# Last quarter of a fused Fourier and state-space kernel: half of its DMAs on a second queue, its products cut in half, an early table load

## The chip, the cores and the metric

The kernel runs on one core of a Trainium2 chip. The metric is device time in microseconds (us) for one launch: three unprofiled runs of the kernel before took 581.99, 582.04 and 582.89 us (median 582.04). Each core has a matrix engine (TensorE, PE in the profile, with its weight loads as PEld), VectorE (DVE), ScalarE (ACT), GpSimd (POOL) and SyncE (SP). SP, ACT and GpSimd can each issue DMAs; SP and ACT issue on queues that the profile calls hardware_dynamic, GpSimd on one that it calls software_dynamic. The same 16 DMA engines carry all of them.

## The reference

Two heads are computed and set side by side in the output (2048 x 1024, float32).

```python
# head A: real part of a two-dimensional DFT of x (2048 x 512)
a = einsum("bsd,ed->bse", x, dft_hid_re)
b = einsum("bsd,ed->bse", x, dft_hid_im)
y = einsum("ts,bse->bte", dft_seq_re, a) - einsum("ts,bse->bte", dft_seq_im, b)
# head B: S4D convolution of u (2048 x 512) with 128 states a channel
P = exp((A * dt)[:, :, None] * pos)            # A complex, 512 x 128 x 2048
K = 2 * einsum("dn,dnl->dl", C, P).real
y = irfft(rfft(u, 2L) * rfft(K, 2L), 2L)[:L] + u * D_skip
```

## The kernel before

Head A (class `Fnet`) is a chain of large matrix products in float32 accuracy: each float32 operand is split into a high and a low part (`hi` on ACT, `lo` on DVE), and three matmuls of 128x128 by 128x512 (hi·hi, lo·hi, hi·lo, line 369) make one **group of three**. 32 groups of three make one of the last output blocks: eight steps k by four column blocks d, and the last two steps of each d stand together, so that its accumulator can be evacuated on ACT (line 394; the very last one half on ACT, half on DVE, lines 387 to 391) and stored as `out_ya`. The moving operands come as tiles `raw` on SP's queue. There are seven `raw` buffers.

Head B (class `Ssm`) builds the convolution kernel K from tables of powers (lines 611 to 640), for 64 channels at a time (n = 0 to 7). `taps` (line 807) makes 64 channels of K, `stage1_k` does the first step of K's transform on PE (line 838), takes its two PSUM banks off with one ACT copy (line 848) and two DVE operations each (850, 852), and `store_k` writes the result `xk_sb` to DRAM as `xk` in four DMAs of 256 KB: two halves a, each with two halves y. Rows of these stores are 256 bytes long, 1024 rows in a store.

The channels are taken in quarters h of 128. For each quarter and each of four parts q, `load_spectrum` loads the spectra of u and K, `product` multiplies by the second transform step on PE (line 1000, 64 matmuls, two halves r = 0, 1 of 32), copies to SBUF on ACT (line 1014, tile `uk`), forms the complex product on DVE (lines 1017 to 1030, tiles `z` and `uk`), applies the first inverse step on PE (line 1037), copies on ACT (line 1052, tile `z`) and stores `zs` to DRAM (line 1061). `inverse2`, which does the last two quarters, loads `zs` back as `zl` (line 1093: one half of the partitions on SP's queue, the other on GpSimd's), adds and subtracts on DVE (lines 1099, 1101), multiplies by the table `ib2` on PE (line 1108), copies on ACT (line 1113) and stores `out_yb` (line 1116).

In the last quarter (h = 3) the spectra don't fit a tile of their own. They are loaded into the buffers of head A's operand x, eight tiles `x_hi` and `x_lo` for each half r of each q; each DMA for K brings 128 KB in rows of 512 bytes, 256 rows. So K's last store (n = 7), the 16 loads `x_hi<-xk`, `x_lo<-xk` (line 973), the four products of h = 3 and the two inverses of h = 3 form the chain that ends the program, with head A's last two output blocks on PE beside it.

The order of all instructions is written out by a planner (`Plan`): each piece of work is a generator that yields the engine and a planned duration, and the planner always takes the piece that can start first, then the one with the smaller urgency number. The engines then follow that order, each in its own queue. DMAs are issued on SP in that order too. Each of SP's DMAs reports to one of eight semaphores, in turn, so one may have to wait until the DMA eight places earlier on its queue has landed. GpSimd's DMAs have eight semaphores of their own.

Names for what follows: K's last stores are `xk<-xk_sb` for n = 7; the spectra loads are `x_hi<-xk` and `x_lo<-xk`; products q = 0 to 3 are those of h = 3.

Of the kernel before, what the change touches and what calls it, by code (L numbers as in the profile page):

```python
# [56 lines left out]
ASKED, APART_BY, COMES = 2.0, 3.8, 2.4  # L57
APART = None, True
LATE = 1, 1, 3, 1


def HELD():
# [135 lines left out]
class Fnet:  # L198
# [60 lines left out]
    def load_x0(self, raw):  # L259

        yield "dma", load(64)
        self.nc.sync.dma_start(raw[:, :128], self.xin[0, :, :128])
        self.x[0] = self.still(0)
        yield "act", act(128)
        self.nc.scalar.activation(self.x[0][0][:, :128], raw[:, :128], AF.Copy)
        yield "dve", dve(128)
        self.nc.vector.tensor_tensor(self.x[0][1][:, :128], raw[:, :128], self.x[0][0][:, :128].bitcast(F32),
                                     op=OP.subtract)
        self.plan.set(self.x0_ev)
# [164 lines left out]
class Ssm:  # L434


    def __init__(self, tc, ctx, plan, fnet, nd, ldt, dsk, uG, f1u, f1k, w2, ia, ib, ib2, out):
        self.tc, self.nc, self.plan, self.fnet = tc, tc.nc, plan, fnet
        self.nd, self.ldt, self.uG, self.ib2_in, self.out = nd, ldt, uG, ib2, out
        self.const = ctx.enter_context(tc.tile_pool(name="b_const", bufs=1))  # L440
        self.fps = ctx.enter_context(tc.tile_pool(name="b_fps", bufs=1, space=PSUM))
        dram = ctx.enter_context(tc.tile_pool(name="b_dram", bufs=1, space=DRAM))
        self.xu = dram.tile([64, 2, 32, DM], F32, name="xu")
        self.xk, self.zs = (dram.tile([4, 64, 2, 32, PART], F32, name=n) for n in ("xk", "zs"))
        self.dt_dram = dram.tile([128, 4], F32, name="dt_dram")
# [3 lines left out]
        self.cst = [[(n, self.const.tile([128, *a.shape[1:]], F32, name=n), a) for n, a in s] for s in (first, second)]  # L449
# [375 lines left out]
    def stage1_k(self, ks, n, ev):  # L825

        nc = self.nc
        yield ev
        yield "dve", dve(16)
        nc.vector.tensor_tensor(ks[:, 0], self.dskip[:, 16 * n:16 * n + 16], ks[:, 0], op=OP.add)  # L830
        yield self.const_ev
        got = yield from self.banks(2)
        yield "pe", 1.11, None, 64
        for a in range(2):
            for j in range(4):
                for y in range(2):
                    r, o = slice(32 * j, 32 * j + 32), 32 * a + 16 * y
                    nc.tensor.matmul(got[j // 2][1][64 * y:64 * y + 64, j % 2, 256 * a:256 * a + 256], self.f1k[r, a],  # L838
                                     ks[r, o:o + 16].rearrange("p l i -> p (l i)"), start=True, stop=True,
                                     tile_position=(32 * j, 64 * y))  # L840
        self.plan.put(self.kss)
        yield self.xks
        xs = self.tab.tile([128, 2, 16, 64], F32, name="xk_sb")
        for h, (k, p) in enumerate(got):
            even, odd = (p[:, :, 256 * a:256 * a + 256].rearrange("p j (l i) -> p j l i", l=16) for a in range(2))
            lo, hi = (xs[:, a, :, 32 * h:32 * h + 32].rearrange("p l (j i) -> p j l i", j=2) for a in range(2))
            yield "act", act(512)
            nc.scalar.activation(hi, odd, AF.Copy)
            yield "dve", dve(512)
            nc.vector.tensor_tensor(lo, even, hi, op=OP.add)  # L850
            yield "dve", dve(512), *APART
            nc.vector.tensor_tensor(hi, even, hi, op=OP.subtract)
            self.give(k)
        xk = self.xk[n // 2].rearrange("(a s) c (y l) d -> y a (s c) l d", a=2, y=2)[..., 64 * (n % 2):64 * (n % 2) + 64]
        left = [2]
        for a in range(2):
            self.plan.spawn(self.store_k(xk, xs, a, n, left), 1)

    def store_k(self, xk, xs, a, n, left):
        yield "dma", load(512, 230), FAST  # L860
        for y in range(2):
            self.nc.sync.dma_start(xk[y, a], xs[64 * y:64 * y + 64, a])
# [105 lines left out]
    def load_spectrum(self, name, h, q, view):  # L968
        yield "dma", load(512, 270), FAST
        for r in range(2):  # L970
            for p, xt in enumerate(self.xt[h, q][r]):
                n = xt.shape[1]
                self.nc.sync.dma_start(xt[:, :, "uk".index(name)], view[2 * q + r, :, n * p:n * p + n])
        self.plan.set(self.xt_ev[name, h, q])

    def products(self):
        for h in range(4):
            yield self.set_ev[h // 3]
            b = self.sets[h // 3]
            for q in range(4):  # L980
                for n in "uk":
                    yield self.xt_ev[n, h, q]
                yield b.uks
                got = yield from self.banks(2)
                done = Event()
                self.plan.spawn(self.product(b, h, q, got, done), LATE[h])
                yield done

    def product(self, b, h, q, got, done):
        nc, v, a = self.nc, self.nc.vector, self.nc.scalar  # L990
        uk = b.pool.tile([128, 2, 2, 2, 2, PART], F32, name="uk", bufs=b.n)
        yield "pe", 1.89, None, 128
        for r in range(2):
            for c in range(2):
                for xx in range(4):
                    xt = self.xt[h, q][r]
                    xt = (xt[xx * len(xt) // 4])[:, xx % (4 // len(xt))]
                    for g in range(2):
# [2 lines left out]
                                         self.w2[rows, 2 * q + r, xx, 32 * c:32 * c + 32],  # L1001
                                         xt[rows].rearrange("p n d -> p (n d)"),
                                         start=True, stop=True, tile_position=(64 * g, 32 * xx))
        if h < 3:
            self.plan.put(b.xts)
        self.plan.set(done)
        u, t = uk[:, :, :, :, 0], uk[:, :, :, :, 1]
        yield b.zbs
        P = b.pool.tile([128, 2, 2, 2, PART], F32, name="z", bufs=b.n)
        left, ready = [2], Event()  # L1010

        def half(r, k, p):
            yield "act", act(1024), HELD
            a.activation(uk[:, r].rearrange("p g c n d -> p g (c n d)"), p, AF.Copy)  # L1014
            self.give(k)
            yield "dve", dve(512)
            v.tensor_tensor(P[:, r], t[:, r], u[:, r], op=OP.mult)  # L1017
            yield "dve", dve(512), *APART
            v.tensor_tensor(t[:, r], t[:, r], u[:, r, :, ::-1], op=OP.mult)  # L1019
            left[0] -= 1  # L1020
            if not left[0]:
                self.plan.set(ready)
        for r in range(2):
            self.plan.spawn(half(r, *got[r]), LATE[h])
        yield ready
        yield "dve", dve(512)
        v.tensor_tensor(u[:, :, :, 0], P[:, :, :, 0], P[:, :, :, 1], op=OP.subtract)
        self.plan.put(b.zbs)
# [38 lines left out]
    def inverses(self, h):  # L1067

        yield self.zs_ev[h]
        if h >= HALVED:  # L1070
            yield self.ib2_ev
        b = self.sets[int(h >= min(HALVED, 3))]
        for i in range(2):
            yield b.zls
            self.plan.spawn((self.inverse2 if h >= HALVED else self.inverse)(b, h, i, 16), 1)

    def load_ib2(self):
        yield self.set_ev[1]
        yield self.zs_ev[1]
        self.ib2 = self.sets[1].pool.tile([128, 16, 2, 32], F32, name="ib2")  # L1080
        yield "dma", load(512)
        self.nc.sync.dma_start(self.ib2, self.ib2_in)
        self.plan.set(self.ib2_ev)

    def inverse2(self, b, h, i, n):
# [5 lines left out]
        for y, e in enumerate((nc.sync, nc.gpsimd)):  # L1091
            o = n * i + c * y
            e.dma_start(z[64 * y:64 * y + 64], view[:, :, o:o + c])
        yield "dma", load(64 * n, 270), FAST
        t = b.pool.tile([128, c, PART], F32, name="zsum", bufs=b.n)
        for w in range(0, c, 4):
            m = slice(w, w + 4)
# [125 lines left out]
```

## Time and profile before

| what | us |
|---|---|
| median of the unprofiled runs | 582.04 |
| the profiled execution's own time | 583.77 |
| its span (first to last instruction) | 581.9 |
| PE busy in the span | 569.9 (98%) |
| PE's last matmul ends | 576.25 |
| K's last first-step matmuls start | 497.22 |
| first of K's last stores issued | 502.68 |
| first and last spectra load of K issued | 509.56, 524.22 |
| products q = 0 to 3 start on PE | 515.50, 521.03, 531.36, 539.55 |

The profile is of one execution. Its "busy" time for PE counts matmuls that are pipelined, so a busy PE can still be short of its peak; small gaps between matmuls don't show as idle. The chain of work is followed back from the last instruction: at each step to what released it. Times in a timeline count from the span's start, and a row with "xN" merges N instructions.

### The profile page before, as it was taken

What the parts mean: (1) busy time and instruction counts of PE and PEld (TensorE: products, weight loads), DVE (VectorE), ACT (ScalarE), POOL (GpSimd) and SP (SyncE); (2) the same over time, 40 slices, a digit from 0 to 9 for tenths busy, and PEclk for the clock granted to TensorE, in tenths of its full rate; (3) what the DMA queues carried; (4) which work ended last, traced back from release to release, by engine and by line L of the source; (5) the groups of instructions that cost most, each with busy time, mean ns of one, the idle gap of its engine ahead of it and who ended that gap; (6) DMA issues with size and microseconds to landing.
All of it is one profiled execution on the core that took longest, in us unless ns stands there. A gap on an engine that the chain in (4) does not pass through costs nothing.

```text
span 581.9 us, 15684 instructions
## 1 busy us (share of the span) xinstructions
PE 569.9 (98%) x6278; PEld 434.2 (75%) x6278; DVE 523.4 (90%) x927; ACT 371.8 (64%) x729; POOL 42.5 (7%) x64
## 2 busy tenths in 40 slices
PE   8999999999999999999999999999999999999996
PEld 5877777788777777778787776777787778766784
DVE  6999999999999999999999999999989999346723
ACT  5678766673777495758569485844688744344622
POOL 0001101100110000000100001001100000000000
PEclk9999999999999999999999999999999999999999
DMA  7998999997469767867796888469999995699886
GB/s 247 326 362 244 289 287 276 275 285 186 118 162 227 205 172 227 203 172 225 206 223 186 227 200 251 131 173 286 258 287 258 229 289 193 157 227 305 236 198 185
DMA packets 147976, 133.70 MB, mean 230 GB/s; under 512 B 47296, under 2 KB 107328, under 8 KB 147648
## 3 DMA queue, kind: packets, MB, share of 16 engines
q1 hardware_dynamic: 138976, 115.54, 66.6%
q0 software_dynamic: 8640, 16.78, 14.5%
q8 instruction: 49, 0.80, 0.6%
q10 hardware_dynamic: 288, 0.39, 0.2%
q14 instruction: 23, 0.19, 0.1%
HBM read 89.95 MB, written 42.73 MB: 228 GB/s over the span
## 4 chain that ended last, share of the span: by engine, by line
PE 55%; DVE 27%; DMA 7%; issue 6%; ACT 3%; SPq 1%; ACTq 0%; DVEq 0%
PE acc L369 42%; DVE prod L611 9%; DVE t L620 5%; PE f L1000 4%; DVE lo L228 4%; PE f L807 3%; PE f L1037 3%; DMA x_hi<-xk 2%; DMA xt<-xk 2%; DVE t L640 1%; DMA xk<-xk_sb 1%; PE f L838 1%; DVE cs L681 1%; DMA zl<-zs 1%; DVE uk L1019 1%
## 5 line engine op out<-in xcount | busy, mean ns | idle before, releaser
L369 PE MATMUL acc<-hi,x_hi 128*128 128x512 f32 x640 | 258.7, 404 | 0.8 <-ACT x_hi L224 0.7
L369 PE MATMUL acc<-lo,x_hi 128*128 128x512 f32 x640 | 250.8, 392 | 0.0
L369 PE MATMUL acc<-hi,x_lo 128*128 128x512 f32 x640 | 250.2, 391 | 0.0
L611 DVE TENSOR_TENSOR prod<-t,cs 128x1024 f32<-128x1024 f32 (+4 forms) x192 | 163.2, 868 | 1.7 <-ACT t L729 0.6
L369 PEld LDWEIGHTS acc<-hi,x_hi 128*128 128x128 f32 x640 | 120.5, 188 | 50.1 <-issue 23.4
L369 PEld LDWEIGHTS acc<-hi,x_lo 128*128 128x128 f32 x640 | 120.7, 189 | 26.4 <-DVE x_lo L228 0.3
L369 PEld LDWEIGHTS acc<-lo,x_hi 128*128 128x128 f32 x640 | 120.8, 189 | 23.1 <-DVE lo L228 0.2
L224 ACT ACTIVATE hi<-raw 128x512 fp32r<-128x512 f32 x132 | 82.7, 628 | 64.8 <-PE acc L369 48.7
L228 DVE TENSOR_TENSOR lo<-raw,hi 128x512 fp32r<-128x512 f32 x132 | 90.2, 686 | 26.9 <-ACT hi L224 26.9
L620 DVE TENSOR_TENSOR t<-prod 128x512 f32<-128x512 f32 (+4 forms) x192 | 94.3, 512 | 1.0
L627 ACT ACTIVATE square<-t 128x256 f32<-128x256 f32 (+1 forms) x64 | 36.7, 573 | 29.1 <-DVE t L620 26.9
L1014 ACT ACTIVATE uk<-f 128x1024 f32<-128x1024 f32 x32 | 31.3, 1018 | 15.0 <-PE f L1000 15.0
L323 POOL DMA_DIRECT2D lo<-in_sT x28 | 24.5, 874 | 214.8 <-ACT lo L321 44.2
L394 ACT ACTIVATE y<-acc 128x512 f32<-128x512 f32 x47 | 28.0, 595 | 16.6 <-PE acc L369 16.4
L807 PEld LDWEIGHTS f<-t,t 128*32 128x32 f32 x2048 | 29.5, 110 | 6.9 <-issue 4.8
L807 PE MATMUL f<-t,t 128*32 128x64 f32 x2048 | 32.4, 220 | 0.9 <-issue 0.4
L318 POOL DMA_DIRECT2D hi<-in_sT x28 | 15.8, 564 | 190.2 <-PE acc L369 119.8
L1017 DVE TENSOR_TENSOR z<-uk 128x512 f32<-128x512 f32 x32 | 21.9, 686 | 6.1 <-ACT uk L1014 6.0
L1052 ACT ACTIVATE z<-f 128x512 f32<-128x512 f32 x32 | 17.8, 592 | 14.5 <-PE f L1037 11.3
L640 DVE TENSOR_TENSOR t<-square 128x128 f32<-128x128 f32 (+1 forms) x64 | 24.7, 387 | 0.0
L1000 PE MATMUL f<-xt,w 64*32 64x256 f32 x768 | 23.5, 379 | 0.3 <-DMA xt<-xk 0.3
L1019 DVE TENSOR_TENSOR uk<-uk 128x512 f32<-128x512 f32 x32 | 22.1, 691 | 0.9
(102 smaller groups left out, 505.0 us busy)
## 6 DMA issues: line engine op xcount, KB each, us to landing
raw<-in_sT SPq DMA_DIRECT2D x99, 256.0 KB, 5.3
p<-y SPq DMA_DIRECT2D x32, 256.0 KB, 3.5
xk<-xk_sb SPq DMA_DIRECT2D x32, 256.0 KB, 5.1
zs<-z SPq DMA_DIRECT2D x32, 256.0 KB, 4.0
raw<-p SPq DMA_DIRECT2D x32, 256.0 KB, 4.2
hi<-in_sT POOLq DMA_DIRECT2D x28, 256.0 KB, 4.7
lo<-in_sT POOLq DMA_DIRECT2D x28, 256.0 KB, 5.0
xt<-xu SPq DMA_DIRECT2D x24, 256.0 KB, 4.8
```

The source lines that it names most:

```text
L224: self.nc.scalar.activation(hi, src, AF.Copy)
L228: self.nc.vector.tensor_tensor(lo, src, hi.bitcast(F32), op=OP.subtract)
L369: nc.tensor.matmul(acc[d], l[:, cols], r, start=k == 0 and n == 0, stop=k == len(items) - 1 and n == 2)
L394: self.nc.scalar.activation(y, ps, AF.Copy, scale=-1.0 if g[2] == 1 else 1.0)
L611: self.nc.vector.tensor_tensor(p.rearrange("p k d c m -> p k (d c) m"), src.rearrange("p d c l -> p (d c) l")[:, None, :, rows].to_broadca ...
L620: self.nc.vector.tensor_tensor(dst[:, :, :, rows], p[:, 0], p[:, 1, :, ::-1], op=OP.add)
L627: self.nc.scalar.activation(sq, t[:, :, :, m // 2:m], AF.Square)
L640: self.nc.vector.tensor_tensor(t[:, :, 0, m:2 * m:2], box[0][:, :, 0], box[0][:, :, 1], op=OP.subtract)
L807: nc.tensor.matmul(ps[32 * j:32 * j + 32, i], t1[:, d, c], t2[:, d, c], start=c == 0, stop=c == 1, tile_position=(0, 32 * j))
L1000: nc.tensor.matmul(got[r][1][32 * xx:32 * xx + 32, g, 256 * c:256 * c + 256], self.w2[rows, 2 * q + r, xx, 32 * c:32 * c + 32], xt[rows].r ...
L1014: a.activation(uk[:, r].rearrange("p g c n d -> p g (c n d)"), p, AF.Copy)
L1019: v.tensor_tensor(t[:, r], t[:, r], u[:, r, :, ::-1], op=OP.mult)
```

## The change

Seven edits, all but the last of them for the program's last part:

- `store_k`: for n = 7 the half y = 1 of each store goes out on GpSimd's queue (two DMAs), the half y = 0 stays on SP's.
- `load_spectrum`: K's spectra for `x_lo` (p = 1, which only h = 3 has) go out on GpSimd's queue, eight DMAs; those for `x_hi` stay on SP's.
- `stage1_k`: for n = 7 the two banks are taken off by two pieces of work with urgency -1 instead of one after the other.
- `product`: for h = 3 the PE work is given to the planner as two halves of 32 matmuls, and the first half's evacuation is spawned before the second half's matmuls.
- `ib2`, the table of `inverse2`, gets a place of its own that it shares with `f1u` (a table that only the first transform of u uses), and is loaded when the last `t1` table is done instead of after quarter 1's inverse steps.
- `inverses`: the inverses of h = 2 and 3 get urgency 2 instead of 1; the planned load of `zl` is no longer preferred for h = 2.
- `load_x0`: the very first copy (`x_hi`, 128 columns) moves from ACT to DVE.

```diff
@@ load_x0
-        yield "act", act(128)
-        self.nc.scalar.activation(self.x[0][0][:, :128], raw[:, :128], AF.Copy)
+        yield "dve", dve(128, 2)
+        self.nc.vector.tensor_copy(self.x[0][0][:, :128], raw[:, :128])
@@ Ssm.__init__
+        self.ib2 = self.const.tile([128, 16, 2, 32], F32, name="ib2")
+        f1u_at = self.ib2.rearrange("p a b c -> p (a b c)")[:, :64]
...
@@ stage1_k
+        xs = []
+
+        def out(h, k, p):
+            if not xs:
+                yield xs_ev
...
+            yield "act", act(512)
+            nc.scalar.activation(hi, odd, AF.Copy)
+            yield "dve", dve(512)
+            nc.vector.tensor_tensor(lo, even, hi, op=OP.add)
+            yield "dve", dve(512), *APART
+            nc.vector.tensor_tensor(hi, even, hi, op=OP.subtract)
+            self.give(k)
+            left[0] -= 1
+            if not left[0]:
+                self.plan.set(ready)
...
         for h, (k, p) in enumerate(got):
...
+            if n < 7:
+                yield from out(h, k, p)
+            else:
+                self.plan.spawn(out(h, k, p), -1)
+        yield ready
@@ store_k
-        for y in range(2):
-            self.nc.sync.dma_start(xk[y, a], xs[64 * y:64 * y + 64, a])
+        for y, e in enumerate((self.nc.sync, self.nc.gpsimd if n == 7 else self.nc.sync)):
+            e.dma_start(xk[y, a], xs[64 * y:64 * y + 64, a])
@@ load_spectrum
-                self.nc.sync.dma_start(xt[:, :, "uk".index(name)], view[2 * q + r, :, n * p:n * p + n])
+                e = self.nc.gpsimd if p and name == "k" else self.nc.sync
+                e.dma_start(xt[:, :, "uk".index(name)], view[2 * q + r, :, n * p:n * p + n])
@@ product
-        yield "pe", 1.89, None, 128
         for r in range(2):
+            if not r or h == 3:
+                yield "pe", 1.89 if h < 3 else 0.95, None, 128 if h < 3 else 64
...
+            if not r and h == 3:
+                self.plan.spawn(half(0, *got[0]), urgency)
@@ inverses
         if h >= HALVED:
             yield self.ib2_ev
+            yield self.set_ev[1]
...
-            self.plan.spawn((self.inverse2 if h >= HALVED else self.inverse)(b, h, i, 16), 1)
+            self.plan.spawn((self.inverse2 if h >= HALVED else self.inverse)(b, h, i, 16), 1 if h < 2 else AFTER)
@@ load_ib2
-        yield self.set_ev[1]
-        yield self.zs_ev[1]
-        self.ib2 = self.sets[1].pool.tile([128, 16, 2, 32], F32, name="ib2")
-        yield "dma", load(512)
+        yield self.t1_ev[15]
+        yield "dma", load(512), FAST
         self.nc.sync.dma_start(self.ib2, self.ib2_in)
@@ inverse2
-        yield "dma", load(64 * n, 270), FAST
+        yield "dma", load(64 * n, 270), FAST if h == 3 else None
```

The planner's order is the same up to some 85 us before the end, but for the moved copy at the start and the load of `ib2` (its tile is called `ib` in the rows). Where it moves, at three places:

SP's queue around K's last stores, before. `x_hi_6013` to `x_lo_6016` are the four loads of q = 0, `6017` to `6020` those of q = 1, and so on:

```order
L862 DMA xk<-xk_sb 64x16x64 x4
L337 DMA raw<-p_1_3_88 128x512
L403 DMA out_ya<-y 128x512
L973 DMA x_hi_6013<-xk 128x2x128
L973 DMA x_lo_6014<-xk 128x2x128
L973 DMA x_hi_6015<-xk 128x2x128
L973 DMA x_lo_6016<-xk 128x2x128
L973 DMA x_hi_6017<-xk 128x2x128
L973 DMA x_lo_6018<-xk 128x2x128
```

The same place on SP's queue now, down to the last of the `x_hi` loads:

```order
L882 DMA xk<-xk_sb 64x16x64 x2
L339 DMA raw<-p_1_2_87 128x512
L339 DMA raw<-p_1_3_88 128x512
L994 DMA x_hi_6013<-xk 128x2x128
L994 DMA x_hi_6015<-xk 128x2x128
L994 DMA x_hi_6017<-xk 128x2x128
L994 DMA x_hi_6019<-xk 128x2x128
L1121 DMA zl<-zs 64x2x1024 x2
L994 DMA x_hi_6021<-xk 128x2x128
L994 DMA x_hi_6023<-xk 128x2x128
L994 DMA x_hi_6069<-xk 128x2x128
L994 DMA x_hi_6078<-xk 128x2x128
```

GpSimd's queue after its last load for head A, now; before, the two pairs of `zl<-zs` stood there alone:

```order
L882 DMA xk<-xk_sb 64x16x64 x2
L994 DMA x_lo_6014<-xk 128x2x128
L994 DMA x_lo_6016<-xk 128x2x128
L994 DMA x_lo_6018<-xk 128x2x128
L994 DMA x_lo_6020<-xk 128x2x128
L1121 DMA zl<-zs 64x2x1024 x2
L994 DMA x_lo_6022<-xk 128x2x128
L994 DMA x_lo_6024<-xk 128x2x128
L994 DMA x_lo_6070<-xk 128x2x128
L994 DMA x_lo_6079<-xk 128x2x128
L1121 DMA zl<-zs 64x2x1024 x2
```

Ten DMAs went from SP's queue to GpSimd's. SP's half of `zl` for h = 2, which stood behind `ib` and an inverse's store, now stands between the spectra of q = 1 and q = 2, as GpSimd's half does on its own queue. One `out_ya` store that stood ahead of the spectra now stands behind them. Product q = 0 stands two groups of three earlier on PE (23 instead of 25 groups after the last first-step matmuls of K), and between the products stand three groups of three where there were four.

ACT where K's two banks are taken off, before:

```order
L224 ACTIVATE hi<-raw 128x512
L848 ACTIVATE xk_sb<-f_6616 128x2x16x16
L224 ACTIVATE hi<-raw 128x512
L848 ACTIVATE xk_sb<-f_6623 128x2x16x16
L224 ACTIVATE hi<-raw 128x512 x2
```

And now:

```order
L226 ACTIVATE hi<-raw 128x512
L846 ACTIVATE xk_sb<-f_6617 128x2x16x16
L846 ACTIVATE xk_sb<-f_6624 128x2x16x16
L226 ACTIVATE hi<-raw 128x512 x3
L396 ACTIVATE y<-acc 128x512 x3
```

The split of a `raw` tile that stood between the two copies now follows them; on DVE the two operations of the second bank move ahead of that split's `lo` in the same way.

The end of ACT's queue, before:

```order
L394 ACTIVATE y<-acc 128x512 x3
L1113 ACTIVATE zl<-f_7416 128x512 x2
L389 ACTIVATE y<-acc 128x256
L391 DMA out_ya<-y 128x256
L1113 ACTIVATE zl<-f_7470 128x512 x2
```

And now:

```order
L1141 ACTIVATE zl<-f_7382 128x512 x2
L1141 ACTIVATE zl<-f_7429 128x512 x2
L396 ACTIVATE y<-acc 128x512 x3
L391 ACTIVATE y<-acc 128x256
L393 DMA out_ya<-y 128x256
```

The last inverse of head B (`zl`) used to be the last work of all; now seven groups of three of head A follow it on PE, and the program ends with the two stores of half an `out_ya` block.

More of the change, by code (lines that the diff above doesn't have):

```diff
@@ L59 @@
 LATE = 1, 1, 3, 1
+AFTER = 2
+LAST = 1
 def HELD():
@@ L448, in __init__ @@
         second = ("w2", w2), ("ia", ia), ("ib", ib)
-        self.cst = [[(n, self.const.tile([128, *a.shape[1:]], F32, name=n), a) for n, a in s] for s in (first, second)]
+        self.ib2 = self.const.tile([128, 16, 2, 32], F32, name="ib2")
+        f1u_at = self.ib2.rearrange("p a b c -> p (a b c)")[:, :64]
+        self.cst = [[(n, f1u_at if n == "f1u" else self.const.tile([128, *a.shape[1:]], F32, name=n), a) for n, a in s]
+                    for s in (first, second)]
         self.halfpi = self.const.tile([128, 1], F32, name="halfpi")
@@ L832, in stage1_k @@
         got = yield from self.banks(2)
+        xs = []
+        def out(h, k, p):
+            if not xs:
+                yield xs_ev
+            even, odd = (p[:, :, 256 * a:256 * a + 256].rearrange("p j (l i) -> p j l i", l=16) for a in range(2))
+            lo, hi = (xs[0][:, a, :, 32 * h:32 * h + 32].rearrange("p l (j i) -> p j l i", j=2) for a in range(2))
+            yield "act", act(512)
[8 more added lines that the diff above has]
+                self.plan.set(ready)
+        xs_ev, ready, left = Event(), Event(), [2]
         yield "pe", 1.11, None, 64
@@ L842, in stage1_k @@
         yield self.xks
-        xs = self.tab.tile([128, 2, 16, 64], F32, name="xk_sb")
+        xs.append(self.tab.tile([128, 2, 16, 64], F32, name="xk_sb"))
         for h, (k, p) in enumerate(got):
[L845 to L853, printed above, removed]
+            if n < 7:
[3 more added lines that the diff above has]
+        yield ready
+        xs, = xs
         xk = self.xk[n // 2].rearrange("(a s) c (y l) d -> y a (s c) l d", a=2, y=2)[..., 64 * (n % 2):64 * (n % 2) + 64]
@@ L985, in products @@
                 done = Event()
-                self.plan.spawn(self.product(b, h, q, got, done), LATE[h])
+                self.plan.spawn(self.product(b, h, q, got, done), LATE[h] if h < 3 else LAST)
                 yield done
@@ L991, in product, with half @@
         uk = b.pool.tile([128, 2, 2, 2, 2, PART], F32, name="uk", bufs=b.n)
-        yield "pe", 1.89, None, 128
+        u, t = uk[:, :, :, :, 0], uk[:, :, :, :, 1]
+        P, left, ready, urgency = [], [2], Event(), LATE[h] if h < 3 else LAST
+        def half(r, k, p):
+            yield "act", act(1024), HELD
+            a.activation(uk[:, r].rearrange("p g c n d -> p g (c n d)"), p, AF.Copy)
+            self.give(k)
+            if not P:
+                yield P_ev
+            yield "dve", dve(512)
+            v.tensor_tensor(P[0][:, r], t[:, r], u[:, r], op=OP.mult)
+            yield "dve", dve(512), *APART
+            v.tensor_tensor(t[:, r], t[:, r], u[:, r, :, ::-1], op=OP.mult)
+            left[0] -= 1
+            if not left[0]:
+                self.plan.set(ready)
+        P_ev = Event()
         for r in range(2):
+            if not r or h == 3:
+                yield "pe", 1.89 if h < 3 else 0.95, None, 128 if h < 3 else 64
             for c in range(2):
@@ L1006, in product @@
         self.plan.set(done)
-        u, t = uk[:, :, :, :, 0], uk[:, :, :, :, 1]
         yield b.zbs
[L1009 to L1024, printed above, removed]
+        P.append(b.pool.tile([128, 2, 2, 2, PART], F32, name="z", bufs=b.n))
+        self.plan.set(P_ev)
+        for r in range(h == 3, 2):
+            self.plan.spawn(half(r, *got[r]), urgency)
         yield ready
+        P, = P
         yield "dve", dve(512)
```

## The prediction

> **What bounds the kernel now.** The page first, then the busy time by stretch (start:end, length, then busy time and count of PE, PEld, DVE, ACT and POOL, PE's granted clock, share of the DMA engines, GB/s), then the chain of waits. PE is busy nearly all the time, so only what PE waits for, and what stands before its first and after its last matmul, can be won.
>
> ```profile
> span 581.9 us, 15684 instructions
> PE 569.9 (98%) x6278; PEld 434.2 (75%) x6278; DVE 523.4 (90%) x927; ACT 371.8 (64%) x729; POOL 42.5 (7%) x64
> ```
>
> ```profile
> 525.06:576.25 51.19, 51.19 (x678) 37.96 (x674) 28.65 (x44) 22.96 (x37) 1.16 (x2) 1.00 0.82 235
> 576.25:581.90 5.65, 0.00 (x1) 0.00 (x0) 0.00 (x0) 1.08 (x2) 0.00 (x0) 0.88 0.70 206
> ```
>
> PE has no hole from 525.06 on, and 5.65 us follow its last matmul. The chain that ended last, by pieces (start, length), shows a hole ahead of that and what the pieces cost undisturbed:
>
> ```profile
> 512.63 11.17 DMA x_hi<-xk
> ...
> 523.93 1.20 PE f L1000 x32
> 525.13 2.99 PE acc L369 x12
> 528.11 1.05 PE f L1037 x32
> 529.16 2.27 PE acc L369 x9
> 531.43 1.89 PE f L1000 x64
> ...
> 547.82 2.02 PE f L1108 x112
> ...
> 553.17 19.32 PE acc L369 x84
> ```
>
> One load of K's spectra took 11.17 us. A product takes 1.89 us, a group of three (19.32 - 2.27) / 25 = 0.682, and a restart of head A costs 2.99 - 4 x 0.682 = 0.26. PE's timeline gives the waits:
>
> ```profile
> 515.50 0.42 PE L1000 MATMUL f<-x_hi,w 64*32 64x256 f32 x4
> 518.08 0.50 PE L369 MATMUL acc<-hi,x_hi 128*128 128x512 f32 x1
> 521.03 0.64 PE L1000 MATMUL f<-x_hi,w 64*32 64x256 f32 x8
> 522.14 0.42 PE L1000 MATMUL f<-x_lo,w 64*32 64x256 f32 x4 [0.47 <-DMA x_lo<-xk]
> 525.06 0.50 PE L369 MATMUL acc<-hi,x_hi 128*128 128x512 f32 x1
> ```
>
> Product q = 0 took 518.08 - 515.50 = 2.58, q = 1 took 4.03; less 1.89 each that is 0.69 + 2.14 = **2.83 us of waiting**, all of it for K's spectra. (Idle rows show less, because matmuls overlap.) Why they are late, by the queues' timelines and by the DMA view of 513.5 to 520 us:
>
> ```profile
> 502.68 4.67 SPq L862 DMA_DIRECT2D xk<-xk_sb  x4
> 507.44 1.06 SPq L337 DMA_DIRECT2D raw<-p  x1
> 509.56 0.37 SPq L973 DMA_DIRECT2D x_hi<-xk  x1
> 517.89 0.48 SPq L973 DMA_DIRECT2D x_hi<-xk  x1
> 522.11 0.36 SPq L973 DMA_DIRECT2D x_lo<-xk  x1
> 511.58 1.26 POOL L1093 DMA_DIRECT2D zl<-zs  x2 [66.27 <-DMA out_ya<-y]
> ```
>
> ```profile
> q0 software_dynamic: 256, 0.97, 69.0%
> q1 hardware_dynamic: 955, 0.46, 31.9%
> ```
>
> GpSimd's two `zl` loads, in rows of 4 KB, enter at 511.58 and take 0.97 of the 1.43 MB of the next 6.5 us; SP's spectra, in rows of 512 bytes, get 0.46 MB (71 GB/s). And SP's last loads wait for the semaphore of the DMA eight places ahead (517.89 to 522.11).
>
> **The change, part by part.**
>
> *K's stores and loads.* ACT and DVE now take both banks off without the split between them:
>
> ```profile
> 498.38 0.60 ACT L848 ACTIVATE xk_sb<-f 128x512 f32<-128x512 f32 x1 [1.05 <-PE f L838]
> 501.97 0.68 DVE L850 TENSOR_TENSOR xk_sb<-f,xk_sb 128x512 f32<-128x512 f32 x1
> DMA to landing us min/median/max: 4.5/4.8/5.2
> ```
>
> (The last row is the landing of K's four last stores, all from SP.) The second copy can start at 498.98; DVE's four operations of about 0.69 then run from 499.0 and the first stores can go at 501.1 instead of 502.68. The split that waits behind them has groups in hand, at no cost. SP's own loads can't start before the `raw` at 507.44, which waits for a buffer that PE's pace frees: 507.9 against 509.56.
>
> GpSimd's price for such DMAs is not in the trace. Its rows are of 128 rows each:
>
> ```profile
> L323 POOL DMA_DIRECT2D lo<-in_sT x28 | 24.5, 874 | 214.8 <-ACT lo L321 44.2 <-DVE prod L611 33.5 <-DVE t L620 32.3
> L1093 POOL DMA_DIRECT2D zl<-zs x4 | 2.4, 608 | 113.1 <-DMA out_ya<-y 66.3 <-DMA zs<-z 46.8
> 559.10 1.27 SPq L1093 DMA_DIRECT2D zl<-zs  x2
> 559.60 1.27 POOL L1093 DMA_DIRECT2D zl<-zs  x2 [46.77 <-DMA zs<-z]
> ```
>
> After the same release GpSimd starts 0.50 later than SP. A store has 1024 rows, a load 256: if its time is fixed, both cost 0.61; if it goes by rows, 4.9 and 1.22. A gain below 0.61 is excluded, since no row is cheaper. The accumulating form costs 0.27 more for as many rows, so part of the time is work per row; I take the middle, 2.5 and 0.85, being nearest to neither. Then GpSimd's stores are written by 501.1 + 0.5 + 2 x 2.5 = 506.6, the first lands near 508 (501.1 + 0.5 + 2.5 is 504.1, and SP's shortest landing of 4.5 less its issue of about 0.6 is 3.9), and the `x_lo` loads of q = 0 and 1 are written at 508.5 to 511.9, landing from 512 on. PE wants them at 515.50 - 2 x 0.682 = 514.1 and, after 1.89 and 2.27, at 518.3. Both queues now have the spectra of q = 0 and 1 ahead of `zl`; only SP's `zl`, which comes free first, can slow the last `x_lo`. Those of q = 2 stand behind 2 MB of `zl` and are wanted at 518.3 + 1.89 + 2.27 + 1.05 + 2.27 = 525.8, against 531.36 before: by the 230 GB/s of the quoted stretch (235), 2 MB from about 513 end near 522, and the last of them land about 526. I keep **1.0 us of waiting** of the 2.83 (0.5 at q = 1, 0.5 at q = 2). With GpSimd's lower price nothing waits; with the upper, see the rivals. Next late is the store `zs` of q = 0, which now stands behind four `raw` loads, and which the copy of q = 1 waits for:
>
> ```profile
> 538.67 1.08 ACT L1052 ACTIVATE z<-f 128x512 f32<-128x512 f32 x2 [2.39 <-DMA zs<-z]
> ```
>
> It waits 2.39 already; the early load of `ib2` takes 512 KB out of its way, so I add nothing.
>
> [...]
>
> *More switches on PE.* Twelve pieces of head B stand between groups instead of ten: 2 x 0.26, and the inverse of 2.02 cut in two costs about 0.1: **+0.6**.
>
> *The end.* Before, PE's end is followed by two copies and 512 KB of `out_yb`; now by half a copy and 128 KB on two queues.
>
> ```profile
> 576.65 1.08 ACT L1113 ACTIVATE zl<-f 128x512 f32<-128x512 f32 x2 [0.56 <-PE f L1108]
> 577.76 0.38 SPq L1116 DMA_DIRECT2D out_yb<-zl  x1
> DMA to landing us min/median/max: 3.2/3.2/3.2
> 575.71 0.38 ACT L389 ACTIVATE y<-acc 128x256 f32<-128x256 f32 x1 [1.01 <-ACT zl L1113]
> DMA to landing us min/median/max: 3.1/3.4/3.8
> ```
>
> The first landing is that last `out_yb`'s, the second that of the two half `out_ya`. `out_yb` lands at 577.76 + 3.25 = 581.0, 0.9 before the span's end. Now: 0.48 (copy and hop) + 3.1 to 3.8 + 0.9 = 4.5 to 5.2 against 5.65: **-0.8**, in -1.15 to -0.45.
>
> *The start and the table.* Nothing. PE's second group waits for a later tile of x, not for the first copy:
>
> ```profile
> 6.92 0.79 PE L369 MATMUL acc<-hi,x_hi 128*128 128x512 f32 x1 [0.66 <-ACT x_hi L224]
> ACT hi L224 <- PE acc L369: 3.1, 3, 1.7
> ```
>
> The last row, of the waits of 483 to 512 us, covers `ib2`: splits there wait for PE, not for their `raw` loads, so 2 us of DMA among those loads is hidden; without that cover it costs its 512 KB, some 2 us.
>
> **Sum.** -(2.83 - 1.0) + 0.6 - 0.8 = -2.0. The profiled execution took 583.77 (span 581.9), the median is 1.73 lower; carried over: 582.04 - 2.0 = **580.0**.
>
> **The rivals.**
>
> *Nothing lands sooner.* The engines are shared, so the earlier places only make PE wait longer, and it leaves the products when it did: only the end is won against the switches, 582.04 + 0.6 - 0.8 = 581.8, no change. For it: 71 GB/s beside `zl`. Against: q = 0 and 1 are now ahead of `zl`.
>
> *GpSimd's writing goes by rows* (slower). Place: the stores `xk<-xk_sb`. Two at 4.9 end at 501.6 + 9.8 = 511.4; four loads at 1.22 are written at 512.6 to 516.3 and land some 3.2 later, as the half stores above, at 515.8 to 519.5. Product q = 0 then waits about 1.8, q = 1 about 1.9, since SP's `zl` runs beside its `x_lo`, and q = 2 about 1, behind a `zl` that starts at 517: 4.7 instead of 2.83, 582.04 + 1.9 + 0.6 - 0.8 = 583.7. It decides against the change from a price of about 4 us a store. For it: the accumulating row. Against: no row shows more than 0.87.
>
> *`zs` of q = 0 lands later than its reader* and product q = 3 waits 1 to 1.5: 581.2, still faster.
>
> **Chances.** Forecast 0.52, `zs` late 0.06, nothing sooner 0.20, by rows 0.22. Less than 0.2% (1.2 us) can't be told from no change here; so faster 0.58, same 0.20, slower 0.22. The range's low end is no wait at all and the better end: 582.04 - 2.83 + 0.6 - 1.15 = 578.7; its high end takes in the row rival at 583.7.
>
> **What would show it.** Right: GpSimd's rows `xk<-xk_sb` at 1 to 3.5 us; products q = 0 and 1 with under 1 us of waiting together, q = 2 near 526; PE's last matmul at about 575 and under 5.2 us behind it. Wrong: those rows near 5 us, or products that start earlier and last longer by as much, or a new wait at q = 2 or q = 3.

## The result and the profile after

The changed kernel is slower: 587.19 us in the median of 13 runs (584.23 to 589.58) against 582.7 us of the kernel before in 13 runs beside it (581.57 to 585.04). The ratio is 1.0064, with a 95% interval of 1.0046 to 1.0083, or some 3.7 us. (Ratios here and below are estimated over all the runs; the quotient of the two medians would be 1.0077, or 4.5 us.)

The profiled execution took 584.23 us, the fastest of the 13. Its page:

```profile
span 582.5 us, 15689 instructions
PE 570.0 (98%) x6278; PEld 433.5 (74%) x6278; DVE 522.9 (90%) x928; ACT 371.3 (64%) x728; POOL 49.7 (9%) x74
```

The spans can't be set side by side as they stand, since PE's matmuls became fast earlier in this execution. PE's timeline of the kernel before, at the start and at the last first step of K:

```profile
10.07 0.61 PE L369 MATMUL acc<-lo,x_hi 128*128 128x512 f32 x1
10.50 0.42 PE L369 MATMUL acc<-hi,x_lo 128*128 128x512 f32 x1
497.22 1.12 PE L838 MATMUL f<-ks,f1k 32*64 32x256 f32 x32
```

The same view of the kernel after:

```profile
5.04 0.40 PE L371 MATMUL acc<-hi,x_lo 128*128 128x512 f32 x1
495.25 1.12 PE L861 MATMUL f<-ks,f1k 32*64 32x256 f32 x32
```

Matmuls of some 0.40 us, where one still took 0.61 at 10.07 before, begin at 5.04 instead of 10.50, and K's last first step comes 1.97 us earlier. From that step to the end of the span it took 581.9 - 497.22 = 84.68 us before and 582.5 - 495.25 = 87.25 us after: 2.57 us more. PE's timeline there shows where:

```profile
512.17 0.64 PE L1039 MATMUL f<-x_hi,w 64*32 64x256 f32 x8
513.39 0.42 PE L1039 MATMUL f<-x_lo,w 64*32 64x256 f32 x4 [0.58 <-DMA x_lo<-xk]
517.54 0.42 PE L1039 MATMUL f<-x_hi,w 64*32 64x256 f32 x4
527.29 0.65 PE L1039 MATMUL f<-x_hi,w 64*32 64x256 f32 x4 [2.21 <-DMA x_hi<-xk]
530.88 0.50 PE L371 MATMUL acc<-hi,x_hi 128*128 128x512 f32 x1
537.70 0.42 PE L1039 MATMUL f<-x_hi,w 64*32 64x256 f32 x4 [1.16 <-ACT z L1081]
```

Products q = 0 to 3 begin at 512.17, 517.54, 527.29 and 537.70. From q = 0 to q = 1 stand 5.37 us, where a run below without a wait there has 4.18: 1.19 us of waiting. Product q = 2 waits 2.21 us for its spectra and then runs from 527.29 to 530.88, 3.59 instead of 1.89 us, its matmuls at 0.65 instead of 0.40 us. Product q = 3 waits 1.16 us. Together 1.19 + 2.21 + 1.70 + 1.16 = 6.26 us, against 2.83 before. The granted clock stands in the windows around that hole, and the last row is what follows PE's last matmul (columns as in the prediction):

```profile
523.66:527.07 3.41, 1.43 (x7) 0.83 (x5) 1.38 (x3) 0.95 (x2) 0.00 (x0) 1.00 1.05 250
527.07:530.49 3.42, 3.19 (x60) 2.18 (x64) 0.00 (x0) 0.80 (x1) 0.00 (x0) 0.50 1.11 352
578.36:582.50 4.14, 0.00 (x0) 0.00 (x0) 0.42 (x1) 0.38 (x1) 0.00 (x0) 0.90 0.57 199
```

From 0.2 us before the hole's end the granted clock was 0.50, for 3.42 us. The end takes 4.14 us instead of 5.65. GpSimd's timeline tells why the first spectra are late:

```profile
499.66 0.90 POOL L882 DMA_DIRECT2D xk<-xk_sb  x1 [56.45 <-DVE xk_sb L848]
507.68 0.87 POOL L882 DMA_DIRECT2D xk<-xk_sb  x1 [7.12 <-issue]
508.54 2.15 POOL L994 DMA_DIRECT2D x_lo<-xk  x3
512.41 0.72 POOL L994 DMA_DIRECT2D x_lo<-xk  x1 [1.72 <-PE acc L371]
513.26 1.22 POOL L1121 DMA_DIRECT2D zl<-zs  x2
```

A store takes GpSimd 0.90 us, but 7.12 us pass before it starts on the second one, and no semaphore of the trace explains them. The last spectra of K are then late for another reason. The DMA issues of 513.4 to 516.7 us, and the queues from 520 to 526 us:

```profile
zl<-zs POOLq DMA_DIRECT2D x2, 512.0 KB, 12.1
x_hi<-xk SPq DMA_DIRECT2D x4, 128.0 KB, 14.3
x_lo<-xk POOLq DMA_DIRECT2D x4, 128.0 KB, 12.6
```

```profile
q0 software_dynamic: 346, 1.19, 88.0%
q1 hardware_dynamic: 339, 0.17, 15.6%
```

128 KB of spectra took 12.6 to 14.3 us to land, behind 2 MB of `zl`. The two queues moved as many packets each (346 and 339), but GpSimd's hold 3.4 KB on average and SP's 0.5 KB: 1.19 against 0.17 MB. The chain of waits joins the rest together:

```profile
517.73 14.08 DMA out_ya<-y
531.82 5.12 DMA zs<-z
537.05 0.60 ACT z L1081
537.70 1.96 PE f L1039 x64
```

`out_ya` stands behind the spectra, the second of SP's two stores `zs` of q = 0 isn't issued before that landing, ACT's copy of q = 1 waits for the store, and product q = 3 for the copy.

### The profile page after: what moved, and what is told of

Same layout as the page of the kernel before. It is cut to its first block, busy times and chain, and to the rows that moved or that the text cites. A ratio compares the mean times of both kernels' runs of the same rounds, so it can differ in the third digit from the quotient of the medians.

```text
span 582.5 us, 15689 instructions
## 1 busy us (share of the span) xinstructions
PE 570.0 (98%) x6278; PEld 433.5 (74%) x6278; DVE 522.9 (90%) x928; ACT 371.3 (64%) x728; POOL 49.7 (9%) x74
## 4 chain that ended last, share of the span: by engine, by line
PE 46%; DVE 37%; issue 7%; DMA 6%; ACT 1%; SPq 1%; DVEq 0%; ACTq 0%
PE acc L371 36%; DVE prod L616 11%; DVE t L625 6%; DVE lo L230 6%; PE f L1039 3%; PE f L812 3%; DMA out_ya<-y 2%; PE f L1066 2%; DVE t L645 2%; DMA xt<-xu 1%; DVE cs L686 1%; DVE x_lo L230 1%; DVE z L1023 1%; DVE uk L1025 1%; DVE zl L928 1%
```

## The experiments

Two theories and a rival stood at the start. **A**: the 2 MB of `zl`, let in ahead of the spectra of q = 2 and 3, cost. **B**: GpSimd's second store waits for room in a memory that its DMAs need (`dynamic_dma_scratch_size`, 2048 bytes in this program), and that delays all behind it. **C**: the loss lies elsewhere, in the edit at the start for one.

**zl behind the last spectra**

```diff
             yield self.set_ev[1]
+        if h == 2:
+            yield self.xt_ev["k", 3, 3]
```

> The kernel after, with the first inverse's load of 2 MB (zl, both queues) let go only when the last of K's spectra is issued; the order of PE's, ACT's and DVE's instructions stays. Theory A (the 2 MB ahead of the spectra of q = 2 and 3 are what costs): the spectra of q = 2 and 3, which took 12 to 15 us from issue to landing, take under 7; the idle 2.21 us before product q = 2 and the slow matmuls behind it go, q = 3 no longer waits 1.16 us; 3 to 4.5 us less than the kernel after, 0.5 to 2 us less than the kernel before (ratio 0.997 to 0.999). Theory B (GpSimd's queue, whose second store was issued only at 507.68, 7.1 us after the first was written, is what costs): that wait stays, so the loss stays; at most 1 us is won, ratio 1.005 or more. Theory C (the loss is spread over the kernel, by the edit at its start or the table's load): as the kernel after, ratio 1.006.

Measured: 586.92 us, ratio 1.007 (1.0045 to 1.0094): nothing won. The spectra issued from 513.9 to 517.4 did land in time; the waits and the chain show who waited instead:

```profile
x_lo<-xk POOLq DMA_DIRECT2D x5, 128.0 KB, 4.5
x_hi<-xk SPq DMA_DIRECT2D x4, 128.0 KB, 3.2
```

```profile
526.86 11.84 DMA zs<-z
539.45 3.67 PE f L1039 x64
```

```profile
534.00:539.40 5.40, 0.16 (x1) 0.00 (x0) 3.22 (x6) 0.59 (x2) 0.00 (x0) 0.80 0.85 266
539.40:546.00 6.60, 6.55 (x81) 3.74 (x89) 3.07 (x5) 3.17 (x5) 0.00 (x0) 0.65 0.44 123
```

The 2 MB now stand ahead of `zs` of q = 0, which took 11.84 us to land; PE stood still for 5.3 us ahead of product q = 3, which then took 3.67 us. A's mechanism held (3.2 and 4.5 us instead of 14.3 and 12.6), its gain did not: whoever is behind the 2 MB pays.

**More memory for GpSimd's DMAs**

```diff
-    nc = bacc.Bacc(..., dynamic_dma_scratch_size=2048)
+    nc = bacc.Bacc(..., dynamic_dma_scratch_size=2240)
```

Names of runs and expectations say 128 (entries) for 2048 bytes and 140 for 2240; what an entry is, no run shows.

> [...] Theory B: the second store is issued at about 500.6 instead of 507.68, the x_lo loads of q = 0 and 1 land up to 4 us earlier, and what stands behind them too; 2 to 4 us less than the kernel after (ratio 0.999 to 1.003). Theory A: the second store may go earlier, but so do the 2 MB of zl, and the spectra of q = 2 and 3 still take over 10 us behind them; at most 1.5 us less than the kernel after (1.004 to 1.007). [...]

Measured: 582.4 us, ratio 0.9983 (0.996 to 1.0005), just under the range of B (0.999 to 1.003): the loss is gone. GpSimd's and PE's timelines:

```profile
499.24 1.77 POOL L882 DMA_DIRECT2D xk<-xk_sb  x2 [55.98 <-DVE xk_sb L848]
505.11 2.84 POOL L994 DMA_DIRECT2D x_lo<-xk  x4 [4.11 <-DMA xk<-xk_sb]
```

```profile
511.94 0.42 PE L1039 MATMUL f<-x_hi,w 64*32 64x256 f32 x4
516.12 0.42 PE L1039 MATMUL f<-x_hi,w 64*32 64x256 f32 x4
524.55 0.42 PE L1039 MATMUL f<-x_hi,w 64*32 64x256 f32 x4 [0.89 <-DMA x_hi<-xk]
533.52 0.42 PE L1039 MATMUL f<-x_hi,w 64*32 64x256 f32 x4 [1.38 <-ACT z L1081]
```

192 bytes more, and both stores go out one after the other in 1.77 us; the 7.12 us were a wait for room in that memory. The spectra of q = 0 and 1 come in time (511.94 to 516.12 is the 4.18 used above). A shows in what is left: 0.89 for q = 2, 1.38 for q = 3.

**All from SP again**

```diff
-        for y, e in enumerate((self.nc.sync, self.nc.gpsimd if n == 7 else self.nc.sync)):
+        for y, e in enumerate((self.nc.sync, self.nc.sync)):
...
-                e = self.nc.gpsimd if p and name == "k" else self.nc.sync
+                e = self.nc.sync
```

> The kernel after, with K's last stores and all spectra issued from SP again; the rest of the change stays, zl on both queues and ahead of q = 2 and 3 included. Theory A: q = 2 and 3 still stand behind 2 MB; PE waits for them 2 to 4 us, ratio 1.003 to 1.008. Theory B: GpSimd has nothing to wait for; the products wait 2.8 us or less in all, the end keeps its 1.5 us, ratio 0.998 to 1.000.

Measured: 587.69 us, ratio 1.0071 (1.0046 to 1.0097), as the kernel after. GpSimd has nothing to wait for here, so B alone is not the cause of the loss. PE's waits from 495 us on:

```profile
PE f L1039 <- ACT z L1081: 2.9, 1, 2.9
PE f L1039 <- DMA x_lo<-xk: 1.5, 1, 1.5
PE f L1039 <- DMA x_hi<-xk: 0.8, 1, 0.8
```

The spectra make product q = 0 wait, beside GpSimd's half of `zl`, and the copy behind `zs` makes q = 3 wait.

**The edit at the start, alone**

```diff
-        self.nc.scalar.activation(self.x[0][0][:, :128], raw[:, :128], AF.Copy)
+        self.nc.vector.tensor_copy(self.x[0][0][:, :128], raw[:, :128])
```

> The kernel before, with the first copy of x (128 columns) on DVE instead of ACT and nothing else. Theories A and B: no difference, ratio 0.999 to 1.001. Theory C, as far as it means this edit: 2 to 4 us longer. If the edit is what opened PE's clock 5.5 us earlier in the profile of the kernel after (full from 5.0 instead of 10.5 us), the first product of K ends about 2 us earlier, and the ratio is 0.997.

Measured: 583.63 us, ratio 1.0002 (0.9981 to 1.0022): C, as to this edit, is out, and the edit is worth nothing. Nor does it set when the matmuls become fast: with it, those of some 0.40 us began at 5.0 to 7.2 us in the profiles of the kernel after, hold_zl, ring_140 and this run, but at 10.9 in that of no_split. This run also shows how the kernel before spreads: the same order of work, and in this execution

```profile
PE f L1000 <- DMA x_lo<-xk: 2.4, 1, 2.4
```

one hole of 2.4 us where the profiled execution of before had 0.7 and 0.5.

**The early table, alone and undone**

A second theory **A2** took A's place: the table that is loaded early lets the last-but-one quarter's inverse ask for `zl` earlier, SP's half moves from behind `zs` of q = 0 to between the spectra of q = 1 and 2, and whatever stands behind it costs. Its rival **D** was the other order of PE's last pieces. Into the kernel before went the early load alone:

```diff
+        self.ib2 = self.const.tile([128, 16, 2, 32], F32, name="ib2")
...
     def load_ib2(self):
-        yield self.set_ev[1]
-        yield self.zs_ev[1]
-        self.ib2 = self.sets[1].pool.tile([128, 16, 2, 32], F32, name="ib2")
-        yield "dma", load(512)
+        yield self.t1_ev[15]
+        yield "dma", load(512), FAST
```

> The kernel before with one part of the change: ib2 in a buffer of its own (f1u in its first 64 words) and loaded when the last t1 is there, so that the last-but-one quarter's inverse may be asked for earlier. SP's half of the 2 MB of zl then stands between the spectra of q = 1 and 2 (behind all of them before). Theory A2 (it is the early zl that costs, whatever queue the spectra use): PE waits 2 us or more for the spectra of q = 2 or 3 or for the store zs of q = 0, with matmuls of 0.65 us behind the longest hole; 2 to 4.5 us longer than before, ratio 1.003 to 1.008. Theory B (GpSimd's full queue): no store goes from GpSimd here, ratio 0.999 to 1.001. Theory D (the other order of PE's pieces: split last products, inverses asked for less urgently): not in this kernel, ratio 0.999 to 1.001.

Measured: 587.25 us, ratio 1.008 (1.0056 to 1.0104): the whole loss, without GpSimd's stores and without the other edits. The waits of PE from 495 us on:

```profile
PE f L1003 <- DMA x_lo<-xk: 1.6, 2, 1.3
PE f L1110 <- DVE zsum L1101: 1.2, 1, 1.2
PE f L1003 <- DMA x_hi<-xk: 0.6, 1, 0.6
PE f L1110 <- DVE zl L1103: 0.5, 2, 0.3
```

2.2 of these 3.9 us are for spectra, where the profile of before has 1.2 in the same view. In this kernel the early table also put the last inverse behind all groups of head A, where PE waits 1.7 us for DVE, so the run is no clean measure of A2. The other way round, the kernel after with the table late:

```diff
     def load_ib2(self):
-        yield self.t1_ev[15]
-        yield "dma", load(512), FAST
+        yield self.set_ev[1]
+        yield self.zs_ev[1]
+        yield "dma", load(512)
```

> The kernel after with the table ib2 loaded where it was before; spectra and stores still split over SP and GpSimd, with 128 entries. SP's half of zl then stands behind the last spectra and behind zs of q = 0. Theory A2: the spectra of q = 2 and 3 land under 9 us after issue; the 4 us lost come back and some of the end's 1.5 us is kept: ratio 0.997 to 1.001. Theory B: GpSimd's second store still waits to 507 or later, ratio 1.003 or more. Theory D: ratio 1.004 or more.

Measured: 583.04 us, ratio 1.0006 (0.9985 to 1.0027): the loss is gone with the early table, though GpSimd's second store still waits 7.0 us. So either step alone, the late table or the larger memory, takes the loss away. The late table also moves the inverse of h = 2 behind the last of the products' inverse steps on PE, which this run doesn't part from the place of `zl`. With all from SP besides:

> As late_table, and stores and spectra all from SP again: what is left of the change is K's last stores without the split between their copies, the start, and the order of PE's last pieces. Theory A2: the products wait 2 to 3 us as before the change, the end is 1.5 us shorter, switches cost 0.6: ratio 0.997 to 0.999. Theory B: the same. Theory D: ratio 1.004 or more, as the kernel after.

Measured: 582.69 us, ratio 0.9999 (0.9982 to 1.0015). This is the rest of the change, D's part included: no loss, against D, and no gain either, where 0.1 to 0.3% was expected.

**The early table kept, zl put behind zs of q = 0, with the larger memory**

```diff
+        if h == 2:
+            yield self.z_ev[3, 0]
...
+        self.plan.set(self.z_ev[h, q])
         self.zs_left[h] -= 1
```

> The kernel after with 140 entries in GpSimd's memory and with zl asked for only once zs of q = 0 is stored; the table still loaded early. SP's half of zl then stands behind the spectra and behind that store, GpSimd's half behind its last x_lo. Theory A2: no wait for the spectra of q = 0 to 3 above 0.5 us in all, and zs of q = 0 lands under 6 us after its issue; 1 to 2.5 us less than the kernel with 140 entries alone: ratio 0.994 to 0.997. Theory B: nothing more to win behind the larger memory, ratio 0.998. Theory D: 0.998.

Measured: 580.79 us, ratio 0.9966 (0.9945 to 0.9986), faster than before. PE's list of waits names none of the spectra, though product q = 0 takes 2.53 us instead of 1.89; against that, 5.5 us again follow its last matmul, as the last inverse moved to three groups from the end.

**Is the rest of the early table's cost its own load?**

> before_early_table with zl asked for only once zs of q = 0 is stored, so that SP's half stands behind that store as in the kernel before; the table is still loaded early. Theory A2 (what costs is zl's place, not the table's own load): the 4 us lost come back, PE waits 2 to 4 us in all as before, ratio 0.998 to 1.002. If the table's own 512 KB among the raw loads cost, or its buffer, 1.004 or more stays.

Measured: 585.22 us, ratio 1.0043 (1.0025 to 1.006): half of the loss comes back, not all, against A2's number. What is left is either the 512 KB or the order of PE's pieces, in which the last inverse is still behind all groups. So one kernel moved the load of the table alone, and no other instruction (the edit against before_early_table):

```diff
         yield self.t1_ev[15]
         yield "dma", load(512), FAST
         self.nc.sync.dma_start(self.ib2, self.ib2_in)
+        yield self.set_ev[1]
+        yield self.zs_ev[1]
+        yield "dma", load(512)
         self.plan.set(self.ib2_ev)
```

> The kernel before with the table ib2 loaded early into its own buffer, but everything that follows from it asked for as before: on SP one DMA of 512 KB moves from behind the last spectra to among the raw loads of 485 us, and no other instruction of any engine changes place. If the table's own load costs (the 1.0043 that stayed with zl behind zs), 1.003 to 1.005. If what stayed there is from the other order of PE's last pieces, 0.998 to 1.001; a little less than before is possible, as 512 KB go from the stretch in which zs of q = 0 is late.

Measured: 583.36 us, ratio 1.0009 (0.9988 to 1.0029): no cost that can be told from none. The rest is thus put down to the order of PE's pieces in that kernel, by exclusion; it wasn't undone by itself.

**What GpSimd's queue is worth with zl out of the way**

> ring_140_zl_behind_zs with stores and spectra all from SP (the larger memory then serves only GpSimd's other loads). It tells what GpSimd's queue is worth with zl out of the way. If the split is worth what late_table against late_table_no_split showed with 128 entries (nothing): 0.996 to 0.998. If the larger memory is what made it worth something: PE waits 2 us or more for the spectra of q = 0 and 1, beside GpSimd's half of zl, and the ratio is 0.999 to 1.001.

Measured: 584.2 us, ratio 1.0028 (1.0008 to 1.0048), above both ranges that were expected. In its profile, the fastest of its 12 executions, PE's waits sum to 1.3 us and 5.3 us follow its last matmul; what makes the others slower is open.

> ring_140_zl_behind_zs with 128 entries as in the kernel after. GpSimd's second store waits for the first one's landing again, at 507 to 509; the first x_lo lands at 513 to 515, product q = 0 waits 0.5 to 1.5 us and GpSimd's half of zl is 3 us later, so that zs of q = 0 lands over 8 us after its issue and product q = 3 waits 1 to 2.5 us, as in late_table: ratio 0.999 to 1.003. If the queue's wait is hidden once zl is in its place: 0.996 to 0.998.

Measured: 583.87 us, ratio 1.0027 (1.001 to 1.0045), as expected; the first `x_lo` waits for the second store, PE 1.3 us for it.

> late_table (1.0006 with 128 entries) with 140 entries. If the larger memory is worth as much as in the other two pairs (1.0064 to 0.9983 and 1.0027 to 0.9966, 0.6 to 0.8%), 0.993 to 0.995. If late_table hid the queue's wait by something else, 0.999 to 1.001.

Measured: 579.2 us, ratio 0.9948 (0.9927 to 0.9969), as expected from adding the two causes. The nine ratios to the kernel before in one table:

| zl and table | GpSimd, 2048 bytes | all from SP | GpSimd, 2240 bytes |
|---|---|---|---|
| early, as in the change | 1.0064 | 1.0071 | 0.9983 |
| table early, zl behind zs of q = 0 | 1.0027 | 1.0028 | 0.9966 |
| table late | 1.0006 | 0.9999 | 0.9948 |

Along each row the first two agree: with 2048 bytes the second queue is worth nothing; 192 bytes more make it worth 0.5 to 0.9% against all from SP. (The middle cell of the second row had 2240 bytes too, so the larger memory won nothing there without the split.) Down each column, from the first row to the last, the early `zl`, with the places of the inverses of h = 2 that go with it, costs 0.35 to 0.7%. In the last column PE's waits agree: 0.89 + 1.38 us in the first row and 0.2 in the last, and 0.35% is 2.0 us. The middle row lies between; in it the last inverse is nearer to the end, which the next run moves.

**The last inverse asked for earlier**

```diff
-AFTER = 2
+AFTER = 0
```

> ring_140_zl_behind_zs with the last quarters' inverses asked for with more urgency (AFTER = 0 instead of 2), by which the last inverse stands four groups of head A before PE's end instead of three. There 5.5 us followed PE's last matmul, against 4.1 with 140 entries alone; 0.3 to 1 us of that should go: ratio 0.994 to 0.997. No change if the end waits for out_ya alone.

Measured: 578.72 us, ratio 0.9939 (0.9917 to 0.9961), faster than both kernels, and within the noise of late_table_ring_140. PE's waits from 495 us on are an empty list, and the end is short again:

```profile
520.00:540.00 20.00, 19.93 (x302) 12.89 (x301) 12.85 (x21) 9.44 (x14) 0.00 (x0) 1.00 0.85 223
572.18:576.50 4.32, 0.00 (x0) 0.00 (x0) 0.42 (x1) 0.38 (x1) 0.00 (x0) 0.93 0.58 189
```

## Why the prediction was wrong

The terms against the two profiled executions (from K's last first step on; PE's own work is the time to its last matmul less the waits, 79.03 - 2.83 = 76.20 before and 83.11 - 6.26 = 76.85 after):

| term | forecast | measured |
|---|---|---|
| waiting in the products, slow matmuls included | 2.83 to 1.0: -1.83 | 2.83 to 6.26: +3.43 |
| switches on PE | +0.6 | +0.65 |
| the end | -0.8 | -1.51 |
| sum | -2.0 | +2.57 |

- **The term that failed is the waiting, and in it the step on q = 2**: its spectra "stand behind 2 MB of `zl`", and "the last of them land about 526", priced at 0.5 us. The step named the right transfer, but divided 2 MB by 230 GB/s as if the spectra came next at full rate. In 520 to 526 us SP's queue moved 0.17 MB, beside 1.19 MB of GpSimd's. The spectra let PE go at 527.29, in the clock of the profile before 529.26: 3.3 us later than forecast, with a hole of 2.21 us.
- **"Next late is the store `zs` of q = 0 ... so I add nothing"** failed: 1.16 us at q = 3 here, and between none and 5.3 in the other orders. The rival of that name gave it 1 to 1.5 us, right in place and size, but as a deduction from a gain that wasn't there.
- **The early table at "nothing"**: right for its own load (1.0009), wrong for what it lets in. The text priced 512 KB and treated the order of `zl` as given. late_table (1.0006) shows that without this edit the change loses nothing; with more room on GpSimd's side (ring_140, 0.9983) it loses nothing either.
- **A hole was priced at its length.** The 2.21 us brought 1.70 us of slow matmuls behind them; no term had a place for that.
- **GpSimd's price per store**, 0.61 to 4.9 with 2.5 taken, was 0.90: the middle was too high, and the rival of writing by rows is out. A load of 256 rows took 0.72, one of 128 rows 0.61, so the row of the accumulating form, which the text read as work per row, said nothing about rows. It was still right that the second store comes late, and wrong why: room in the memory (7.12 us of waiting at 2048 bytes, none between the stores at 2240), not writing. With room, both stores are written by 501.0 (499.24 + 1.77), and the 0.5 us kept for q = 1 would have been nothing.
- **The rival "nothing lands sooner"** is what late_table and late_table_no_split measured for the split (1.0006 and 0.9999), but its reason, that shared engines leave nothing to win, is out: with room in the memory the same split wins 0.5 to 0.9%. What wins there is not settled: SP took 4.67 us to issue the four stores before and 1.30 for its two after, and no run tells this saving from the loads' places in the queues.
- **The switches** came out as forecast, but +0.65 is a remainder and not a measurement of its own. **The end** was better than its range: the two halves of `out_ya` landed in 2.4 and 2.1 us, against the 3.1 to 3.8 taken; that the queues were emptier is likely, not shown.
- That the profiles show 2.57 and the runs 3.7 us is not settled: the profiled execution of after was the fastest of its 13, and that of before, at 583.77, slower than its median.

## What to carry to other kernels

A load that is made early to free a wait releases everything that waited with it: list what the planner may now ask for, and where those transfers stand in each queue, before the load is called free. Moving the 2 MB of `zl` behind the last spectra, with the DMA engines full (a share of 0.99 to 1.05 from 515.5 to 526 us after the change), only changed who waited: product q = 2 for 2.21 us in the kernel after, q = 3 for 5.3 in hold_zl. So put a bulk transfer behind the last small transfer that the busiest engine needs, and price a hole on TensorE at its length plus the slow matmuls that may follow (2.21 + 1.70 us here). Before moving DMAs to GpSimd, compare the memory that they need there with what is to be in flight (7.12 us between two stores with 2048 bytes, none with 2240).

## What the runs showed of the hardware

- **GpSimd's DMAs needed room.** With 2048 bytes two 256 KB stores of 1024 rows didn't go out together: 7.12 us between them; with 2240 both went out in 1.77 us. The wait ended 0.4 us after the store ahead had landed. The landings of the two stores in the kernel after:

```profile
xk<-xk_sb POOLq DMA_DIRECT2D x1, 256.0 KB, 7.6
xk<-xk_sb POOLq DMA_DIRECT2D x1, 256.0 KB, 4.4
```

The first landed at 499.66 + 7.6 = 507.26, and GpSimd started on the second at 507.68. That one landed at 507.68 + 4.4 = 512.1, and GpSimd started on the fourth `x_lo`, whose wait of 1.72 us the timeline puts down to PE, at 512.41. In ring_140 the four `x_lo` went out in one row, from 505.11 to 507.95. The other runs with 2048 bytes and the split have the wait too: their chains show 7.89 us of "issue" there in hold_zl, 7.00 in late_table and 7.82 in zl_behind_zs_128. How much of the memory a store or a load takes was not shown.
- **GpSimd's queue moved larger packets.** In 520 to 526 us the queues moved 346 packets of 3.4 KB beside 339 of 0.5 KB. The size of GpSimd's was not that of the rows. In 509 to 513 us GpSimd's queue held only K's second store and `x_lo` loads, in rows of 256 and 512 bytes, while SP's moved `x_hi` in rows of 512:

```profile
q0 software_dynamic: 200, 0.61, 64.9%
q1 hardware_dynamic: 811, 0.39, 32.8%
```

That is 3 KB a packet for GpSimd and 0.5 KB for SP. So `x_lo` also changed its packets when it changed its queue; no run prices this apart. Packets were as many on both queues in 520 to 526 us (346 and 339), where GpSimd's took seven times the bytes, but not in 509 to 513 us nor in the prediction's 513.5 to 520 (811 to 200, 955 to 256).
- **One hole was followed by a low clock on PE, a longer one was not.** The hole of 2.21 us in the kernel after was followed by a granted clock of 0.50, for 3.42 us. One of 2.54 us in late_table was not, by PE's timeline and the window:

```profile
537.47 0.42 PE L1039 MATMUL f<-x_hi,w 64*32 64x256 f32 x4 [2.54 <-ACT z L1081]
```

```profile
537.00:541.00 4.00, 3.54 (x71) 2.86 (x72) 1.12 (x2) 3.19 (x5) 0.00 (x0) 1.00 1.03 225
```

In hold_zl, with a hole of 5.3 us, the clock was 0.80 from 534.0 to 539.4 us and 0.65 from 539.4 to 546.0. What decides between them was not shown.
